# Fused attention, gated attention and mixer on one core: value products in fewer runs on parts of TensorE's array

## The chip, the cores and the metric

One NeuronCore of a Trainium2 chip runs the whole program. The metric is the device time of one execution in microseconds. A profiled execution also gives a trace, in which TensorE is called PE (its weight loads PEld), VectorE DVE, ScalarE ACT, GpSimd POOL and SyncE SP. All times of the trace count from the start of its span.

## The reference, cut to what matters

Three stages on 4 batches of 768 tokens, all in float32:

```python
# 1: attention in chunks of 32 queries, 8 heads of 64, context 16 left, 8 right, 8 memory tokens
scores = scale * np.matmul(q_c, k_full.transpose(0, 1, 3, 2))
a = softmax(scores);  out[:, :, c_start:c_end] = np.matmul(a, v_full)
# 2: 4 causal "expert" heads of 64 on x (768 x 512), each token keeps 2 of them by a gate
q = x @ wq[e];  k = x @ wk[e];  v = x @ wv[e]
a = softmax(where(causal, -1e9, scale * (q @ k.transpose(0, 2, 1))))
ye = a @ v @ wo[e];  out += mask * w * ye
# 3: mixer over tokens of rank 32, then a two-layer net 512 -> 2048 -> 512 with relu
u = x + (x.transpose @ U @ V).transpose;  return u + relu(u @ w_ch1) @ w_ch2
```

## The kernel before, in words

The program has an attention part (stages 1 and 2 and the mixer) and a dense part (the two-layer net). The change is in the attention part. The order of all instructions is made by a planner at build time: it takes the program's order as priorities and keeps a model of the engines' times. `tc.high_priority(AHEAD)` moves instructions up in that order.

**Local units.** Stage 1 is cut into 32 units (batch, pair of heads, half of the tokens). A unit is loaded by `local_load` (q_t, k_t, v_t on SP's queue), scored twice for three groups by `local_scores` (L533) and, one round later, turned by `local_turn` (L561, copied into `at` tiles at L563). `local_values` then makes its products with v_t, 12 calls that are 24 instructions of 64 columns each, and `local_split` copies the 128x384 result out of PSUM as xh (ACT) and xl (DVE), both at L580. These are the inputs of the projections of the next batch half.

**Rounds.** Stage 2 goes batch by batch through 12 rounds (list ROUNDS): a pair of expert heads pr and a block i of 128 queries, i = 0 to 2 for both pairs, then 3 to 5 for both. `rnd` writes one round: the load and the scores of a new unit, `scores` of the new block (L672, L674), `turn_scores` of the block before (transposes at L750, copied into `ath` tiles at L753), and one or two fillers. Fillers are `qk_proj` (L592), `v_proj` (L632), `mix_turn` (L778), `mix_up` (L808). Each round then ends in a "session": `local_values` of the unit turned in this round, `values` of the block turned in this round (products with v, 64 columns; in the first rounds of batch 0 and one of batch 3, by the table DELAY, of the block before it), and in some rounds `mix_down` (32 columns). All these matmuls are recorded by the helper `part` at L828, so that all have one line. The list `session` chains them in order and makes the first one wait for all copies that any of them reads. Behind it `keep` (L768) copies a block's 128x128 result into yT, and `mix_keep` the mixer's. `s_at` says in which round a unit is loaded, FILL and FILL0 how many fillers a round has.

**PSUM.** A tag is a set of PSUM tiles used in turn. Of the 8 banks of 2 KB, scores, transposes of scores and mix_turn use tag c (two tiles of two banks), local scores and turns tag lt (two banks), a session's results tag ts (one bank), and projections, mix_up and some spare tiles tag q (one bank). In a session's bank the unit's result stands in the first 384 columns and the block's in the last 128.

```python
TL, TE, TQ = dict(tag="lt", bufs=2), dict(tag="ts", bufs=1), dict(tag="q", bufs=1)
```

**The last batch** has no local units. Its rounds are filled by the first weights of the dense part and by `early`: two chunks of the dense net (`gemm1` L365, `gemm2` L382), whose results po stand in tags lt and q by turns.

Of the kernel before, what the change touches and what calls it, by code (L numbers as in the profile page):

```python
# [8 lines left out]
F32 = mybir.dt.float32  # L9
# [25 lines left out]
HALF = S // 2  # L35
# [4 lines left out]
WLOAD = {1: ((0,), ()), 2: ((1,), ()), 3: ((2, 3), ()), 5: ((), (0, 1))}  # L40
# [8 lines left out]
NKB = 2  # L49
NVB = 3  # L50
NLWK = 4
NLT = 3
NLA = 1
NAT = 6
DELAY = {0: (0, 1, 2, 3, 4, 5, 6, 7, 8), 3: (0,)}
NXP = 8
FS = 1
HG = 1
# [45 lines left out]
def tile_chunk_attention__moe_attention__mixer(  # L104
# [287 lines left out]
    def early(ps):  # L392

        for c in range(NEC):
            load_z(c)
            for f in range(FA):
                gemm1(ps, c, f, TL)
                yield
            for m in range(KT):
                po = ps.tile([128, 512], F32, name="po", **(TL if m % 2 else TQ))  # L400
                for f in range(FA):
                    gate = GATES.get(2 * m + f // 2) if c == NEC - 1 else None
                    with tc.issue_after(hold[gate]) if gate else ExitStack():
                        gemm2(po, c, f, m, f == FA - 1, f == 0)
                    if f % 2:
                        yield
                save_part(po, c, m)
            for f in range(FA):
                hs.pop((c, f))

    TC = dict(tag="c", bufs=2)
    TL, TE, TQ = dict(tag="lt", bufs=2), dict(tag="ts", bufs=1), dict(tag="q", bufs=1)
    ROUNDS = [(pr, i) for hf in range(2) for pr in range(2) for i in range(3 * hf, 3 * hf + 3)]
    with ExitStack() as p1:
        const = p1.enter_context(tc.tile_pool(name="const", bufs=1))
# [150 lines left out]
        def local_values(u, po):  # L566
            w = half[u]
            for qd in range(2):
                at = w["at"].pop(qd)
                for n in range(3):  # L570
                    g = qd * 3 + n
                    for j in range(2):
                        part(po[j * 64:(j + 1) * 64, g * GQ:(g + 1) * GQ], w["v"][:, g, j, :],
                                         at[:, n, j * 64:(j + 1) * 64], start=True, stop=True)
# [162 lines left out]
        turned_ins = {}  # L737
# [91 lines left out]

        def rnd(new=None, old=None, s_unit=None, o_unit=None, fill1=(), fill2=(), down=None, then=None, late=()):
            if s_unit:
                local_load(s_unit)
                if then:
                    load_weights(*then)
                local_scores(s_unit, 0)
            turned = []

            def between():  # L840
                if o_unit:
                    local_turn(o_unit, 0)
                turned.append(1)
            if new:
                scores(*new, between)
            if not turned:
                between()
            if s_unit:
                local_scores(s_unit, 1)
            if o_unit:  # L850
                local_turn(o_unit, 1)
            for f in fill1:
                f()
            if old:
                turn_scores(*old)
            for f in fill2:
                f()
            t = ps.tile([128, 512], F32, name="t", **TE) if o_unit or late else None
            places = [t[:, HALF:], t[:, :128]] if late else []
            with tc.high_priority(AHEAD):  # L860
                session.clear()
                behind = [x for v in late for x in turned_ins.pop(v)] + (half[o_unit]["ins"] if o_unit else [])
                if down:
                    pq = t if not o_unit else ps.tile([128, 512], F32, name="pq", **TQ)
                    behind += ys_ins.pop(down[:2])
                if o_unit:
                    local_values(o_unit, t[:, :HALF])
                for v, p in zip(late, places):
                    values(*v, p)
                if down:  # L870
                    mix_down(*down, pq)
                for x in behind:
                    tc.add_manual_dep(session[0], x.name, READY, reason="start of a run on parts of the array")
                for x, y in zip(session, session[1:]):
                    tc.add_manual_dep(y, x.name, QUEUE, reason="run on parts of the array")
            for v, p in zip(late, places):
                keep(*v, p)
            if o_unit:
                local_split(o_unit, t[:, :HALF])
            if down:  # L880
                mix_keep(*down, pq)

# [51 lines left out]
        for r in range(PRO):  # L934
            more = [lambda: qk_begin(0, 0, r - 2, pp)] if 2 <= r < KT + 2 else []
            if r == PRO - 1:
                more += [lambda t=t: v_proj(0, t) for t in range(3)]
            split = [lambda: split_weights(*WSPLIT[r])] if r in WSPLIT else []
            rnd(s_unit=units[r], o_unit=units[r - 1] if r else None, fill1=split, fill2=more, then=WLOAD.get(r))
            if r == 3:  # L940
                fetch_mixer()
            if r == 4:
                nc.vector.memset(rank_s, 0.0)
                nc.sync.dma_start(identb_s, identb)
                nc.sync.dma_start(tri_s, tri)
                nc.vector.memset(row_s[:, :S - 128], 0.0)
                nc.vector.tensor_copy(row_s[:, S - 128:], tri_s)
        load_mixer()
        old, mixed, turned = None, {}, []
        for b in range(B):  # L950
            last = b == B - 1
            s_at = {} if last else dict(zip(S_AT0 if b == 0 else S_AT, batch_half(b + 1, 0) + batch_half(b + 1, 1)))
            before = None
            if b == 0:
                s_at.update(zip(range(8), units[PRO:]))
                before = units[PRO - 1]
            work = pieces(b, 1) + ([] if last else pieces(b + 1, 0))
            for r, (pr, i) in enumerate(ROUNDS):
                n = (FILL0 if b == 0 else FILL)[r] if work else 0
                ending[0] = last and r >= 10  # L960
                now, work = work[:n], work[n:]
                f1, f2 = now[:1], now[1:]
                if b and r == (2 if last else 1):
                    f2 = f2 + [lambda: mix_turn(b - 1, 1)]
                if b and r == (4 if last else 7):
                    f1 = [lambda: mix_up(b - 1, 1)] + f1
                if r == 10:
                    f2 = f2 + [lambda: mix_turn(b, 0)]
                if b and r == 0 and not mixed.get(b - 1):
                    f1 = [lambda: mix_up(b - 1, 0)] + f1  # L970
                down = (b, 0) if r == 11 else (b - 1, 1) if b and r == 3 else None
                wait = r in DELAY.get(b, ())
                late = turned if wait or not old else turned + [old]
                turned = [old] if wait and old else []
                rnd((b, pr, i), old, s_at.get(r), s_at.get(r - 1) if r else before, f1, f2, down, late=late)
                old = (b, pr, i)
                if last:
                    if r == 0:
                        close_local()
                        behind_x.append(17)  # L980
                        with tc.issue_after(hold['q', 16]):
                            load_wt()
                        fuse = fuse_w1(ps, 0, TL)
                        fetch_w1()
                    if r < 6:
                        with tc.issue_after(hold['q', 16]) if r < 2 else ExitStack():
                            take(fuse, 2)
                    if r == 1:
                        fetch_w2()
                    if r == 3:  # L990
                        take(fuse, 99)
                        fuse_g = fill()
                    if 3 <= r < 6:
                        take(fuse_g, 1)
                    if r == 5:
                        close_proj()
            if last:
                rnd(None, old, late=[old])
                mix_turn(b, 1)
                mix_up(b, 0)  # L1000
                session.clear()
                pq = ps.tile([128, 512], F32, name="pq", **TE)
                mix_down(b, 1, pq)
                mix_keep(b, 1, pq)
                mix_up(b, 1)
                take(fuse_g, 999)
# [256 lines left out]
```

## Time and profile before

| | us |
|---|---|
| median of 3 runs | 819.76 (819.11 to 821.08) |
| profiled execution, whole | 821.44 |
| its span, first to last instruction | 819.0 |
| mean granted clock of TensorE | 0.994 |
| TensorE busy in the span | 794.0 |
| VectorE, ScalarE, GpSimd busy | 620.1, 499.4, 160.8 |

In a timeline a row is a group of like instructions: start, length from its first start to its last end, engine, line, tiles written and read, the weights' rows*columns, the shape, the count. A bracket gives the idle time ahead of it and what ended it. Matmuls overlap in the array: the start of each is recorded, its end is modelled, so one that follows closely starts before the end of the one before.

### The profile page before, as it was taken

Reading aid. Unit: us, or ns where it says so; the run is one execution under the profiler, and the core shown is the slowest. Engines: PE = TensorE matmul, PEld = TensorE weight load, DVE = VectorE, ACT = ScalarE, POOL = GpSimd, SP = SyncE. Lnnn points to the kernel's source line nnn. Section 1 sums busy time; section 2 is a strip of 40 time slices with the busy share of each in tenths; the row PEclk is TensorE's granted clock in tenths of the full one; section 3 lists DMA queues with packets and bytes.
Section 4 is the critical chain, followed back from the end, with each engine's and each line's share of the span. In section 5 each row is a group of like instructions: output and inputs, shape, how many; then the busy total and the mean of one; then the engine's idle time right before and its main releaser. Section 6 shows DMA issues by size and latency. Waiting matters only on the chain.

```text
span 819.0 us, 17878 instructions
## 1 busy us (share of the span) xinstructions
PE 794.0 (97%) x6382; PEld 713.1 (87%) x6382; DVE 620.1 (76%) x2029; ACT 499.4 (61%) x1448; POOL 160.8 (20%) x244
## 2 busy tenths in 40 slices
PE   8989999999999998999999999999999999999997
PEld 5779999798989897888788888999999999999996
DVE  6687767977767759959758799989587595885956
ACT  6787667776667646656445667665455564654652
POOL 4554443634233333422000000000000000000000
PEclk9999999999999999999999999999999999999999
DMA  9443343333223004123427635103003021030211
GB/s 290 128 139 110 101 128 95 122 106 95 67 89 106 27 9 185 62 94 112 142 77 242 196 129 180 53 1 111 19 2 129 1 93 37 1 130 1 78 52 52
DMA packets 36792, 77.67 MB, mean 95 GB/s; under 512 B 4192, under 2 KB 12896, under 8 KB 35936
## 3 DMA queue, kind: packets, MB, share of 16 engines
q1 hardware_dynamic: 36416, 76.21, 28.6%
q8 instruction: 50, 0.82, 0.4%
q14 instruction: 38, 0.31, 0.1%
q10 hardware_dynamic: 288, 0.32, 0.1%
HBM read 60.79 MB, written 15.73 MB: 93 GB/s over the span
## 4 chain that ended last, share of the span: by engine, by line
PE 75%; DVE 13%; ACT 5%; DMA 4%; issue 3%; POOL 0%; DVEq 0%; ACTq 0%; SPq 0%
PE acc L1136 24%; PE ph L365 15%; PE t L828 7%; PE pqk L592 6%; PE po L382 4%; PE tpc L750 4%; PE pv L632 4%; PE s L533 3%; DMA raw<-in_w 2%; PE sc L672 2%; PE sc L674 2%; PE tp L561 2%; DVE d_t L143 1%; ACT a L540 1%; DVE d_t L144 1%
## 5 line engine op out<-in xcount | busy, mean ns | idle before, releaser
L1136 PE MATMUL acc<-xhi,sw 128*128 128x256 f32 x1008 | 187.9, 282 | 0.1
L1136 PEld LDWEIGHTS acc<-xhi,sw 128*128 128x128 f32 x1008 | 159.3, 189 | 4.8 <-ACT xhi L1054 0.3
L1136 PE MATMUL acc<-xlo,sw 128*128 128x256 f32 x504 | 139.1, 282 | 0.2 <-DVE xlo L1055 0.2
L1051 DVE TENSOR_TENSOR sx<-t 128x256 f32<-128x256 f32 x180 | 67.7, 421 | 67.0 <-ACT t L1044 66.9
L1044 ACT ACTIVATE t<-ph 128x512 f32<-128x512 f32 x72 | 43.1, 598 | 100.5 <-PE ph L365 100.5
L1136 PEld LDWEIGHTS acc<-xlo,sw 128*128 128x128 f32 x504 | 95.5, 190 | 2.4 <-DVE xlo L1055 0.4
L730 POOL TENSOR_SCALAR ac<-ac,su,g 128x128 f32<-128x128 f32 (+5 forms) x92 | 70.4, 774 | 129.8 <-DVE su L728 73.9
L1054 ACT CAST xhi<-sx 128x256 fp32r<-128x256 f32 x205 | 74.8, 406 | 21.7 <-DVE sx L1051 19.0
L540 ACT ACTIVATE a<-a,nm 128x96 f32<-128x96 f32 x192 | 69.9, 366 | 15.7 <-DVE nm L537 15.2
L1055 DVE TENSOR_TENSOR xlo<-sx,xhi 128x256 fp32r<-128x256 f32 x205 | 76.7, 420 | 3.0 <-ACT xhi L1054 2.2
L695 ACT ACTIVATE ac<-ac,nmc 128x128 f32<-128x128 f32 (+5 forms) x72 | 47.8, 665 | 24.1 <-DVE nmc L693 23.7
L365 PE MATMUL ph<-zh,wp_l 128*128 128x512 f32 x192 | 61.4, 398 | 0.0
L365 PE MATMUL ph<-zh,wp_h 128*128 128x512 f32 x192 | 60.8, 394 | 0.0
L545 POOL TENSOR_TENSOR a<-a,rs 128x288 f32<-128x288 f32 x64 | 43.3, 679 | 76.3 <-DVE rs L544 12.7
L750 PE MATMUL tpc<-ident_s,ac 128*128 128x128 f32 x336 | 54.2, 286 | 3.5 <-DVE nmc L693 1.4
L533 PE MATMUL s<-k_t,q_t 128*128 128x96 f32 (+1 forms) x480 | 52.7, 272 | 3.9 <-DMA k_t<-in_kw 1.1
L365 PE MATMUL ph<-zl,wp_h 128*128 128x512 f32 x176 | 55.5, 394 | 0.0
L533 PEld LDWEIGHTS s<-k_t,q_t 128*128 128x128 f32 (+1 forms) x480 | 46.5, 174 | 9.1 <-issue 4.0
L750 PEld LDWEIGHTS tpc<-ident_s,ac 128*128 128x128 f32 x336 | 40.1, 146 | 11.4 <-issue 3.5
L693 DVE CUSTOM_DVE_ANT_0 ac<-sc,row_s 128x128 f32<-128x128 f32 (+5 forms) x72 | 42.8, 620 | 9.4 <-PE sc L674 8.5
L672 PE MATMUL sc<-kl,qs 128*128 128x384 f32 (+2 forms) x144 | 47.3, 334 | 2.1 <-DVE zf L354 1.0
L537 DVE CUSTOM_DVE_ANT_0 a<-s,band_s 128x96 f32<-128x96 f32 x192 | 39.4, 250 | 10.8 <-PE s L533 10.2
(209 smaller groups left out, 1950.2 us busy)
## 6 DMA issues: line engine op xcount, KB each, us to landing
raw<-in_w SPq DMA_DIRECT2D x42, 256.0 KB, 3.7
v_t<-in_vw SPq DMA_DIRECT2D x32, 288.0 KB, 3.3
q_t<-in_qT SPq DMA_DIRECT2D x24, 384.0 KB, 3.2
k_t<-in_kw SPq DMA_DIRECT2D x31, 220.0 KB, 3.5
part<-o SPq DMA_DIRECT2D x24, 256.0 KB, 3.1
pt<-part SPq DMA_DIRECT2D x6, 1024.0 KB, 4.8
out<-pt SPq DMA_DIRECT2D x24, 256.0 KB, 2.3
raw<-in_w SPq DMA_DIRECT2D x11, 512.0 KB, 4.0
```

Of the source, the lines that this page charges most:

```text
L365: nc.tensor.matmul(p, w[f // 4][:, pr, fs], z[:, pr], start=(n == 0), stop=(n == 5))
L533: last = nc.tensor.matmul(s[own, j, :], w["q"][own, qd * 3 + j], k_g[own], start=True, stop=True).ins
L540: nc.scalar.activation(a[:, j, :], a[:, j, :], AF.Exp, bias=nm[:, j:j + 1], scale=-1.0, accum_out=ss[:, j:j + 1])
L592: nc.tensor.matmul(p, w[:, kt, m * 128:(m + 1) * 128], x[b, kt, hf], start=(n == 0), stop=(n == 11))
L672: nc.tensor.matmul(s[:, o:o + w], q, kl[b, e, hf][:, :w], start=True, stop=False)
L730: (nc.vector if ending[0] else nc.gpsimd).tensor_scalar(aa[h][:, :n], aa[h][:, :n], su[:, h:h + 1], gates[b, i // 3][:, i % 3, 2 * pr + h: ...
L750: hold['t', 6 * (i // 3) + 3 * pr + i % 3] = nc.tensor.transpose(tp[h][:, j * 128:(j + 1) * 128], aa[h][:, j * 128:(j + 1) * 128], ident_s ...
L828: session.append(nc.tensor.matmul(*a, **kw).ins)
L1051: nc.vector.tensor_tensor(x, t[:, p[0], p[1]], t[:, q[0], q[1]], op=op)
L1054: nc.scalar.copy(hi, x)
L1055: nc.vector.tensor_sub(lo, x, f32(hi))
L1136: ended[0] = nc.tensor.matmul(acc[n][:, m], w[:, ms], x, start=(f == FA and u == 0 and m == 0), stop=(f == NF - 2 and u == 2 and m == 1)).ins
```

## The change

Sessions no longer stand in every round. A table SESSIONS says which rounds of a batch have one. Units that were turned since the last session are gathered in `locs`, blocks in `turned`; a session takes them together, up to two units and three blocks, and a block that was turned in the session's own round is left for the next one, except in the rounds of the table FRESH. A session with two units, or with a unit and more than one further product, takes two banks. Tags ts and q become one tag of two banks, which sessions, projections, mix_up and spare tiles use in turn. po of `early` now uses tag lt alone. There are 8 ath tiles in place of 6 and 5 at tiles in place of 3. The mix_turn of the batch before moves from round 1 to round 2.

```diff
-NLT = 3
+NLT = 5
-NAT = 6
-DELAY = {0: (0, 1, 2, 3, 4, 5, 6, 7, 8), 3: (0,)}
+NAT = 8
+SESSIONS = {0: (0, 2, 4, 6, 8, 9, 11), 1: (1, 3, 5, 7, 9, 11), 2: (1, 3, 5, 7, 9, 11), 3: (1, 3, 5, 7, 9, 11)}
+FRESH = ((0, 9), (1, 9), (2, 9), (3, 9), (3, 11))
...
-                po = ps.tile([128, 512], F32, name="po", **(TL if m % 2 else TQ))
+                po = ps.tile([128, 512], F32, name="po", **TL)
...
-    TL, TE, TQ = dict(tag="lt", bufs=2), dict(tag="ts", bufs=1), dict(tag="q", bufs=1)
+    TL, TE, TQ = dict(tag="lt", bufs=2), dict(tag="ts", bufs=2), dict(tag="ts", bufs=2)
...
-            t = ps.tile([128, 512], F32, name="t", **TE) if o_unit or late else None
-            places = [t[:, HALF:], t[:, :128]] if late else []
+            if not (locs or late or down):
+                return
+            free = [ps.tile([128, 512], F32, name="t", **TE)]
+            if len(locs) == 2 or locs and len(late) + bool(down) > 1:
+                free.append(ps.tile([128, 512], F32, name="t2", **TQ))
+            pos = [x[:, :HALF] for x in free[:len(locs)]]
+            places = [x[:, o:o + 128] for n, x in enumerate(free) for o in ((HALF,) if n < len(locs) else (HALF, 256, 128, 0))]
             with tc.high_priority(AHEAD):
                 session.clear()
-                behind = [x for v in late for x in turned_ins.pop(v)] + (half[o_unit]["ins"] if o_unit else [])
+                behind = [x for v in late for x in turned_ins.pop(v)] + [x for u in locs for x in half[u]["ins"]]
                 if down:
-                    pq = t if not o_unit else ps.tile([128, 512], F32, name="pq", **TQ)
                     behind += ys_ins.pop(down[:2])
-                if o_unit:
-                    local_values(o_unit, t[:, :HALF])
-                for v, p in zip(late, places):
-                    values(*v, p)
+                kept = [(v, places.pop(0)) for v in late]
+                for n in range(max(len(locs), 1)):
+                    if locs:
+                        local_values(locs[n], pos[n])
+                    for v, p in kept[n:n + 1] if n + 1 < len(locs) else kept[n:]:
+                        values(*v, p)
                 if down:
+                    pq = places.pop(0)
                     mix_down(*down, pq)
...
-            for v, p in zip(late, places):
+            for v, p in kept:
                 keep(*v, p)
-            if o_unit:
-                local_split(o_unit, t[:, :HALF])
+            for u, p in zip(locs, pos, strict=True):
+                local_split(u, p)
...
-                if b and r == (2 if last else 1):
+                if b and r == 2:
                     f2 = f2 + [lambda: mix_turn(b - 1, 1)]
...
-                wait = r in DELAY.get(b, ())
-                late = turned if wait or not old else turned + [old]
-                turned = [old] if wait and old else []
-                rnd((b, pr, i), old, s_at.get(r), s_at.get(r - 1) if r else before, f1, f2, down, late=late)
+                o_unit = s_at.get(r - 1) if r else before
+                locs += [o_unit] if o_unit else []
+                now, wait = turned, [old] if old else []
+                if (b, r) in FRESH:
+                    now, wait = now + wait, []
+                if r in SESSIONS[b]:
+                    rnd((b, pr, i), old, s_at.get(r), o_unit, f1, f2, down, late=now, locs=locs)
+                    turned, locs = wait, []
+                else:
+                    rnd((b, pr, i), old, s_at.get(r), o_unit, f1, f2)
+                    turned = turned + [old] if old else turned
```

## Rows read from the trace of the kernel before

**Rows 1.** The page: TensorE's busy time, and the chain that ended last, by engine.
```profile
PE 794.0 (97%) x6382; PEld 713.1 (87%) x6382; DVE 620.1 (76%) x2029; ACT 499.4 (61%) x1448; POOL 160.8 (20%) x244
...
PE 75%; DVE 13%; ACT 5%; DMA 4%; issue 3%; POOL 0%; DVEq 0%; ACTq 0%; SPq 0%
```

**Rows 2.** Stretches: bounds, length, busy time of each engine, clock, DMA share, GB/s.
```profile
125.00:215.00 90.00, 86.98 (x860) 79.98 (x859) 68.97 (x316) 63.35 (x231) 39.89 (x60) 0.98 0.34 104
215.00:312.00 97.00, 93.71 (x926) 85.99 (x925) 68.37 (x287) 63.15 (x202) 34.54 (x55) 0.98 0.20 65
```

**Rows 3.** PE's timeline: the first and the last of the runs of L828.
```profile
13.94 0.92 PE L828 MATMUL t<-at,v_t 96*64 96x64 f32 x24
...
418.92 0.85 PE L828 MATMUL pq<-y,u_s 128*32 128x128 f32 x12
```

**Rows 4.** PE's timeline: into a run and out of it into a projection.
```profile
267.21 0.28 PE L672 MATMUL sc<-kl,qs 128*128 128x256 f32 x1
267.33 0.28 PE L674 MATMUL sc<-kd,qs 128*128 128x256 f32 x1
267.54 0.92 PE L828 MATMUL t<-at,v_t 96*64 96x64 f32 x24
...
269.04 0.97 PE L592 MATMUL pqk<-xl,wqk_h 128*128 128x384 f32 x4
269.85 0.87 PE L592 MATMUL pqk<-xh,wqk_h 128*128 128x384 f32 x4
```

**Rows 5.** PE's timeline: a run of value products alone, and mix_down by itself.
```profile
136.42 1.53 PE L828 MATMUL t<-ath,vt 128*64 128x128 f32 x24
137.88 0.33 PE L750 MATMUL tpc<-ident_s,ac 128*128 128x128 f32 x1
138.05 0.49 PE L561 MATMUL tp<-ident_s,a 128*96 128x128 f32 x3
...
139.11 0.85 PE L828 MATMUL pq<-y,u_s 128*32 128x128 f32 x12
```

**Rows 6.** Timeline of all engines: the end of a run and the emptying of its bank.
```profile
207.39 1.48 PE L828 MATMUL t<-ath,vt 128*64 128x128 f32 x24
...
208.80 0.39 PE L632 MATMUL pv<-wvg_h,xl 128*128 128x260 f32 x1
...
208.92 0.27 ACT L768 COPY yT<-t 128x128 f32<-128x128 f32 x1
...
209.08 0.48 ACT L580 CAST xh<-t 128x384 fp32r<-128x384 f32 x1
...
209.60 0.56 DVE L580 TENSOR_TENSOR xl<-t,xh 128x384 fp32r<-128x384 f32 x1 [1.55 <-ACT xh L580]
```

**Rows 7.** PE's waits, 40 to 420 us: who, for what, total us, times, longest.
```profile
PE pz L808 <- DVE qs L612: 1.0, 2, 0.5
...
PE pz L808 <- DVE z L809: 0.8, 2, 0.7
PE t L828 <- DVE ath L753: 0.8, 3, 0.3
PE t L828 <- ACT ath L753: 0.6, 1, 0.6
...
PE pqk L592 <- DVE qs L612: 0.2, 1, 0.2
```

**Rows 8.** Stretches where the granted clock falls; the columns of rows 2.
```profile
194.00:196.00 2.00, 1.76 (x10) 1.51 (x10) 2.00 (x10) 1.49 (x5) 0.00 (x0) 0.71 0.50 72
196.00:198.00 2.00, 2.00 (x12) 2.00 (x11) 1.88 (x8) 1.98 (x7) 1.10 (x2) 0.50 0.78 298
...
284.00:286.00 2.00, 2.00 (x11) 2.00 (x11) 1.19 (x3) 1.64 (x4) 0.00 (x0) 0.50 0.00 0
```

**Rows 9.** PE's timeline: mix_up's two products, with the idle time ahead of each.
```profile
281.96 0.41 PE L808 MATMUL pz<-v_st,qm 96*128 96x384 f32 x1 [0.55 <-DVE qs L612]
283.02 0.45 PE L808 MATMUL pz<-v_st,qm 96*128 96x384 f32 x1 [0.65 <-DVE z L809]
```

More of the change, by code (lines that the diff above doesn't have):

```diff
@@ L828, in part, with rnd @@
             session.append(nc.tensor.matmul(*a, **kw).ins)
-        def rnd(new=None, old=None, s_unit=None, o_unit=None, fill1=(), fill2=(), down=None, then=None, late=()):
+        def rnd(new=None, old=None, s_unit=None, o_unit=None, fill1=(), fill2=(), down=None, then=None, late=(), locs=()):
             if s_unit:
@@ L938, in tile_chunk_attention__moe_attention__mixer @@
             split = [lambda: split_weights(*WSPLIT[r])] if r in WSPLIT else []
-            rnd(s_unit=units[r], o_unit=units[r - 1] if r else None, fill1=split, fill2=more, then=WLOAD.get(r))
+            rnd(s_unit=units[r], o_unit=units[r - 1] if r else None, fill1=split, fill2=more, then=WLOAD.get(r), locs=units[r - 1:r] if r else ())
             if r == 3:
@@ L948, in tile_chunk_attention__moe_attention__mixer @@
         load_mixer()
-        old, mixed, turned = None, {}, []
+        old, mixed, turned, locs = None, {}, [], []
         for b in range(B):
@@ L960, in tile_chunk_attention__moe_attention__mixer @@
                 ending[0] = last and r >= 10
-                now, work = work[:n], work[n:]
-                f1, f2 = now[:1], now[1:]
-                if b and r == (2 if last else 1):
+                f1, f2, work = work[:n][:1], work[:n][1:], work[n:]
+                if b and r == 2:
                     f2 = f2 + [lambda: mix_turn(b - 1, 1)]
@@ L997, in tile_chunk_attention__moe_attention__mixer @@
             if last:
-                rnd(None, old, late=[old])
+                rnd(None, old, late=turned + [old])
                 mix_turn(b, 1)
```

## The prediction

> **What bounds the kernel now.** The page comes first. TensorE (PE) is busy 97% of the span and the chain that ended last is 75% PE, 13% VectorE (DVE), 5% ScalarE (ACT) [rows 1]: time goes only if PE has less to do or waits less. Next comes the table of stretches: in the two middle batches DVE works 68.97 of 90 us and 68.37 of 97 us [rows 2], so it can't hide everything that is moved onto it. PE itself is idle there for 3.0 and 3.3 us only, so there is little waiting to win; the list of PE's waits between 40 and 420 us, the attention part, which is all that the change touches, names it [rows 7]. What can be won must lie inside PE's "busy" time; for that, third, I read PE's timeline instruction by instruction, by starts, since ends are modelled. The value products (L828) use 64 or 32 columns of the array; what stands around them in the rounds uses 128. In the timeline they stand in 55 unbroken runs, of which the first and the last are shown [rows 3].
>
> **What a run costs at its two ends.** Going in: between two 128-column score products of 256 columns the distance is 0.12 us (267.21 to 267.33), from the last of them to the run 0.21 (267.33 to 267.54) [rows 4]: +0.09. First pair: 24 value products at the head of a run take 1.53 us [rows 5], 24 that follow local products inside a run 1.48 [rows 6]: +0.05. Going out: in the latter run the last product started 0.27 us (its own length) before the end of the row, at 208.60, and the next full product at 208.80, 0.20 later [rows 6]; inside the run the distance from pair to pair is (1.48 - 0.28) / 11 = 0.109, all but 0.01 of it behind the second of a pair: +0.10. First product after it: four pqk products take 0.97 us just after a run and 0.87 otherwise [rows 4], +0.10; where transposes follow, the first takes 0.17 (137.88 to 138.05) against (0.49 - 0.27) / 2 = 0.11 [rows 5], +0.06. So one run costs 0.30 to 0.34 us beyond its products, on the engine that sets the end.
>
> **The change part by part.** *Fewer runs.* Before, there are 5 runs in the prologue, 47 in the rounds (round 0 of the last batch has none), 2 at the end; the trace has one more because batch 0's mix_down stands alone at 139.11 [rows 5]. After: 5, then 7 + 6 + 6 + 6 = 25, then 2, that is 32. The products are the same ones. 23 runs fewer x 0.325 = -7.5 us (bounds: 23 x 0.30 = 6.9 and 23 x 0.34 = 7.8, if all of it reaches the end). A second local unit behind value products in one run has no switch: both use 64 columns, and the join local-to-value is already inside today's runs.
>
> *One tag of two banks in place of two tags of one.* Today projections, mix_up and spare tiles share one bank. PE's waits for that bank to be emptied are pz on DVE qs 1.0 us, pz on DVE z 0.8, pqk on DVE qs 0.2 [rows 7]: 2.0 in all. With two banks the next tile takes the other one: -1.6, a fifth left for the times when a run has the other one (bounds -2.0 and 0).
>
> *New waits for banks.* By the lists SESSIONS and FRESH, 17 of the 25 runs take both banks (those with two local units, or one and two or more other products). A projection that comes right behind such a run must now wait until a bank is empty; today it has its own. The run whose value products start at 207.39 shows the size: its matmuls end at 208.87, pv starts at once in its own bank, and the run's bank is empty at 209.60 + 0.56 = 210.16 [rows 6], 1.29 us later. Worst case 17 x 1.29 = 21.9 us. Against it: the first of two banks is read while the second is filled, so at the end of the run it is nearly empty; and PE has transposes, scores and local scores of the next round in other banks. The nearest rows are those of the single bank today: by the code 64 tiles go through it in the rounds (28 pqk, 24 pv, 12 pz) and cost 2.0 us of waiting, 0.03 each [rows 7]. I take 0.12 per two-bank run, four times that because two banks go at once: +2.0 (bounds 0 and 21.9).
>
> *Waits at the head of a run.* Products of a round are now mostly taken one or two rounds late, so their copies are long done. Today PE waits for them 0.8 + 0.6 us [rows 7]; round 9 and the last one keep the old order: -0.5 (bounds -1.4 and 0).
>
> *More bunched emptying.* A two-bank run leaves two xh and two xl and up to three yT copies at a time on ACT and DVE (0.48, 0.56 and 0.27 us [rows 6]) where two rounds shared them. The sum of work is the same. Where DVE is already full, 2.00 of 2.00 us at 194 to 196 [rows 8], PE's gain turns into waiting; of the 7.5 us I let a tenth go: +0.7 (bounds 0 and 3.0, if in the two middle batches with 12 of the 23 runs three quarters of a run's price were lost).
>
> *po takes both banks of the tag lt.* It had a bank of the projections' tag for every other tile. One po is 12 products of about 0.23 us, 2.7 us, and its emptying lies beside the next one's filling: at 512 columns about 0.48 x 512 / 384 = 0.64 us, an estimate from the 384-column copy [rows 6]. 8 tiles, +0.3 (bounds 0 and 8 x 0.64 = 5.1). *mix_turn a round later, eight ath and five at tiles:* all copies stay, the consumer mix_down is still in round 3, and the loads of v_t, now held up to two rounds, have three tiles in rounds of some 7.5 us (12 rounds in about 90 [rows 2]): 0. If a tile of v_t came free late, its load would hold the next q_t and k_t behind it on SP's queue, and PE would wait at local scores; [rows 7] has no such wait today.
>
> Sum: -7.5 - 1.6 + 2.0 - 0.5 + 0.7 + 0.3 = -6.6 us. The profiled execution took 821.44 us (819.0 span, 2.4 around it) and would take 814.8. It lies 1.7 above the median of the runs, 819.76, which gives 819.8 - 6.6 = 813.2.
>
> **The Trainium skill against the change.** The rows say that a run's bank is empty 1.29 us after its end and that PE goes on meanwhile [rows 6]. The Trainium skill, page "TensorEngine Tiling (Array Packing)", section "PSUM Bottleneck", says that parts of the array speed up the matmuls but not the emptying of PSUM, so that the copies can become the bound. By that rule longer runs with two banks would stand behind their copies. Today's trace does not show it: the view of [rows 7] has no wait of PE for yT, xh or xl. It is the rule behind the next two rivals.
>
> **Rivals.** *Eaten.* Each two-bank run costs PE 0.45 us of waiting for a bank: 17 x 0.45 = 7.7 in place of 2.0, total -0.9, 818.9. For it: projections do stand right behind runs now [rows 4, 6]. Against: the other banks' work. Chance 0.14.
>
> *Slower.* The same place, with the price that a busy bank had at its worst: pz waited 0.65 us for it at 283.02 [rows 9]. 17 x 0.65 = 11.1, less the other terms' -8.6: +2.5, 822.3. It decides from 8.6 / 17 = 0.51 us per run. For it: this wait was with one bank taken, here it is both. Against: it stood where DVE was overloaded, and occurred twice in 12 pz. Chance 0.14.
>
> *The clock too.* The granted clock is 0.50 at 196 to 198 and at 284 to 286 us [rows 8], 1.2 in place of 2.4 GHz, the second time just after PE had been idle for the pz waits (0.55 and 0.65 us, at 281.96 and 283.02 [rows 9]). At half clock 2.0 us and, at a mean of 0.71, another 2.0 x 0.29 / 0.5 = 1.2 us: 3.2, half of it lost, 1.6 each. If the second bank takes these waits away and the clock stays up, -3.2 more: 810.0. Against: DVE is full there anyway, and a new wait can lower the clock elsewhere. Chance 0.12.
>
> *It doesn't do what it says.* The chain that orders a run forbids nothing in between: batch 0's mix_down was torn off its run [rows 5]. If ten of the 25 runs break in two because their second bank comes late, 13 switches go in place of 23: 3.3 less gain, 816.5. Chance 0.10.
>
> **How the numbers follow.** Forecast 0.50, own range 811 to 815.8. About 0.2% (1.6 us) is what a measurement can tell from none, so faster means under 818.1, slower over 821.4. Faster: 0.50 + 0.12 + 0.10 and a little of "eaten", 0.73; same 0.13; slower 0.14. The range for 8 in 10 takes in the clock's case below and "eaten" above: 809.0 to 820.5; "slower" is left out, with the far end of the clock's case.
>
> **What would show it.** Right: 32 or 33 runs of L828, each with the same prices at its ends; the last run, at 418.92 now [rows 3], earlier by 5 to 8 us, the part behind it as long as before; pz waits gone. Wrong: PE waiting on xl, xh or yT at pqk or pv; runs cut in two; new stretches of 0.50 in the clock. If the runs are 32 and the time has not moved, the price of a run's ends was covered by waits on DVE, and my reading by starts was wrong.

## The result, and the profile after

The changed kernel takes 813.89 us (median of 5 runs, 811.13 to 814.40) against 819.76 before (5 runs): 5.9 us less by the medians, ratio 0.9912 with a 95% interval of 0.9886 to 0.9938. The forecast was 813.2. The profiled execution took 814.0, its span 811.9 against 819.0.

The page of the changed kernel, the lines of [rows 1]:

```profile
PE 784.9 (97%) x6382; PEld 710.2 (87%) x6382; DVE 620.5 (76%) x2029; ACT 497.2 (61%) x1448; POOL 159.4 (20%) x244
...
PE 70%; DVE 16%; ACT 6%; DMA 5%; issue 3%; POOL 0%; DVEq 0%; ACTq 0%; POOLq 0%; SPq 0%
```

The count of PE's instructions is the same, 6382, and PE's busy time is 9.1 us shorter. Where it went shows best when the span is cut at three events: the first score product of batch 0, the first mask product of the last batch (L680, in the kernel before L679), and the last product on parts of the array. Stretches of the kernel before, with the columns of [rows 2]:

```profile
46.41:313.38 266.97, 257.68 (x2582) 237.46 (x2579) 197.47 (x894) 186.27 (x650) 110.60 (x171) 0.99 0.31 96
313.38:419.50 106.12, 102.23 (x738) 84.01 (x737) 82.15 (x171) 61.08 (x145) 26.14 (x33) 1.00 0.31 106
419.50:818.97 399.47, 393.10 (x2600) 359.53 (x2595) 309.10 (x808) 220.47 (x531) 0.00 (x0) 1.00 0.23 80
```

The same stretches of the changed kernel:

```profile
46.49:305.32 258.83, 251.16 (x2590) 234.78 (x2587) 196.91 (x885) 183.98 (x648) 110.46 (x174) 0.99 0.32 95
305.32:412.68 107.36, 100.41 (x730) 84.35 (x729) 83.23 (x173) 61.40 (x145) 25.16 (x30) 1.00 0.33 115
412.68:811.88 399.20, 392.97 (x2600) 359.35 (x2594) 308.86 (x808) 220.30 (x531) 0.00 (x0) 1.00 0.23 80
```

Batches 0 to 2 became 8.1 us shorter, the last batch 1.2 us longer, and the part behind it kept its length. The last run ends 6.8 us earlier (419.50 to 412.68), as forecast. The number of runs is not as forecast: PE's timeline has 44 runs of L829 (L828 before), not 32. Twelve of the 17 two-bank runs stand in two pieces. One of them, in the timeline of the changed kernel (PE's rows, and the last read of the projection pv that stood in the tag before this run):

```profile
74.01 0.92 PE L829 MATMUL t<-at,v_t 96*64 96x64 f32 x24
74.75 0.61 PE L829 MATMUL t<-ath,vt 128*64 128x128 f32 x8
...
74.90 0.16 DVE L636 COPY lg<-pv 128x4 f32<-128x4 f32 x1
...
75.29 0.54 PE L562 MATMUL tp<-ident_s,a 128*96 128x128 f32 x3
75.58 0.42 PE L673 MATMUL sc<-kl,qs 128*128 128x384 f32 x1
...
76.19 0.51 PE L751 MATMUL tpc<-ident_s,ac 128*128 128x128 f32 x3
76.54 0.36 PE L534 MATMUL s<-k_t,q_t 128*128 128x96 f32 x2
76.83 0.92 PE L829 MATMUL t<-at,v_t 96*64 96x64 f32 x24
77.58 0.83 PE L829 MATMUL t<-ath,vt 128*64 128x128 f32 x12
```

The session of round 4 of batch 0 starts with its first unit and block, then transposes and scores come in for 1.5 us, then the second unit and block follow: two entries and two exits, as two separate sessions would have. Yet in this execution the second bank was not late: pv had been read out at 75.06, before the row of the first half ended (75.36). It is the same in seven of the twelve: every earlier tile of the tag had been emptied before the first half ended; in two more it took up to 0.3 us longer, in three 1.2 to 3.5 us. The order was fixed at build time by the planner, on its own model of the times. Why that model put other work between the halves of those seven is not shown.

PE's waits of the changed kernel, 40 to 420 us, with the columns of [rows 7]:

```profile
PE tpc L751 <- POOL ac L731: 2.6, 4, 1.2
PE tpc L751 <- DVE nmc L694: 1.2, 2, 1.1
PE t L829 <- DVE y L782: 1.2, 2, 0.9
...
PE pz L809 <- DVE qm L799: 1.1, 2, 0.6
...
PE t L829 <- DVE ath L754: 0.4, 2, 0.3
...
PE t L829 <- DVE qs L613: 0.3, 1, 0.3
```

The waits of pz for the bank of another tile (DVE qs and DVE z in [rows 7]) are gone, as forecast; pz now waits for its own input qm. No wait for xl, xh or yT, which the prediction had named as a sign of being wrong, is in the list. In the attention part the granted clock fell to half once (170.3 to 173.7 us) in place of twice.

### The profile page after: what moved, and what is told of

Read it like the earlier page. It is cut to its first block, busy times and chain, and to the rows that moved or that the text cites. A ratio compares the mean times of both kernels' runs of the same rounds, so it can differ in the third digit from the quotient of the medians.

```text
span 811.9 us, 17863 instructions
## 1 busy us (share of the span) xinstructions
PE 784.9 (97%) x6382; PEld 710.2 (87%) x6382; DVE 620.5 (76%) x2029; ACT 497.2 (61%) x1448; POOL 159.4 (20%) x244
## 4 chain that ended last, share of the span: by engine, by line
PE 70%; DVE 16%; ACT 6%; DMA 5%; issue 3%; POOL 0%; DVEq 0%; ACTq 0%; POOLq 0%; SPq 0%
PE acc L1150 25%; PE ph L366 14%; PE t L829 6%; PE pqk L593 5%; PE pv L633 3%; PE s L534 3%; PE po L383 3%; PE tpc L751 3%; DMA raw<-in_w 2%; PE sc L673 2%; PE sc L675 2%; PE tp L562 2%; ACT a L541 2%; DVE d_t L144 1%; DMA part<-o 1%
```

## The experiments

All are timed against the kernel before on the same chip; kernels of one block shared a chip. The number of runs is that of the order of PE's instructions.

| kernel | runs | median us | ratio to before, 95% |
|---|---|---|---|
| changed | 44 | 813.89 | 0.9912 (0.9886 to 0.9938) |
| e1_tags | 55 | 838.46 | 1.0225 (1.0205 to 1.0245) |
| e2_group | 44 | 848.45 | 1.0346 (1.0325 to 1.0367) |
| e3_every | 56 | 815.62 | 0.9950 (0.9934 to 0.9967) |
| e4_price | 55, 25 of them interrupted | 830.83 | 1.0127 (1.0109 to 1.0145) |
| e5_whole | 32 | 816.69 | 0.9972 (0.9958 to 0.9985) |
| e6_po | 45 | 828.78 | 1.0111 (1.0088 to 1.0135) |
| e7_tags_po | 54 | 819.32 | 0.9995 (0.9981 to 1.0010) |
| e8_late | 53 | 825.59 | 1.0080 (1.0059 to 1.0101) |
| e9_last | 51 | 811.14 | 0.9892 (0.9869 to 0.9915) |
| e10_first | 49 | 816.49 | 0.9960 (0.9944 to 0.9976) |
| e11_sizes | 55 | 815.56 | 0.9948 (0.9929 to 0.9967) |
| changed_again | 44 | 813.18 | 0.9919 (0.9897 to 0.9941) |

Already the first two columns say that the count of runs alone doesn't order the times: 32 runs are slower than 51.

**First block: what is a run's end worth, and which part of the change holds the gain?**

e1_tags is the kernel before with

```diff
-    TL, TE, TQ = dict(tag="lt", bufs=2), dict(tag="ts", bufs=1), dict(tag="q", bufs=1)
+    TL, TE, TQ = dict(tag="lt", bufs=2), dict(tag="ts", bufs=2), dict(tag="ts", bufs=2)
```

> The kernel before with one edit: tags ts and q become one tag of two banks. Sessions stay as they were, 55 runs of L828. Theory A (the gain is the ends of the runs that went, 0.30 to 0.34 us each): no run goes, so only the waits for the projections' bank can go, at most 2.0 us: 817.8 to 819.8. Theory B (the gain is the second bank for projections and mix_up, and the half-clock stretches that follow their waits): most of the gain is here, 814 to 816.

Both theories missed: 838.46. Its stretches from the last batch on:

```profile
308.81:413.02 104.21, 85.31 (x636) 70.17 (x635) 76.61 (x163) 54.61 (x135) 24.35 (x31) 0.93 0.24 82
413.02:837.77 424.75, 417.53 (x2700) 379.66 (x2696) 317.36 (x819) 227.21 (x541) 0.00 (x0) 1.00 0.24 80
```

The last batch ends early, but it holds 636 matmuls in place of 738, and PE is idle 18.9 us of it (104.21 - 85.31); the part behind has 100 matmuls more and is 25 us longer. Dense work that filled the gaps of the last batch was pushed behind it.

e2_group is the changed kernel with the two old tags (the edit above undone).

> The changed kernel with its tags as before: ts and q are two tags of one bank each, a session's second bank comes from q. The order of its instructions has 44 runs, as the changed kernel's. Theory A: 11 runs fewer than before x 0.325 = 3.6 us and the rest of what the changed kernel won by fewer waits at heads of runs: 814 to 816.5. Theory B: without the common tag the gain is gone, 818.5 to 820.5.

848.45, far worse than either. PE's waits of this kernel, 40 to 420 us:

```profile
PE pqk L593 <- DVE z L810: 4.8, 3, 2.1
PE t L829 <- DVE kl L619: 4.7, 2, 2.3
```

Projections wait for a bank that mix_up holds, and sessions for one that a projection holds. In batches 0 to 2 PE is idle for 28.9 us, in the changed kernel for 7.7. So these two-bank sessions need the common tag; one-bank groups with the old tags were not run.

e3_every is the changed kernel with

```diff
-SESSIONS = {0: (0, 2, 4, 6, 8, 9, 11), 1: (1, 3, 5, 7, 9, 11), ...
+SESSIONS = {b: tuple(range(12)) for b in range(4)}
```

> The changed kernel with a session in every round (SESSIONS holds all 12 rounds): one unit and the block of the round before, no grouping; common tag, eight ath and five at tiles, po on lt stay. 56 runs in its order. Theory A: no run goes, 818.5 to 820.5. Theory C (the gain is that value products come a round late and find their copies done, and that the tags are common): 813.5 to 816.

815.62: with 56 runs, one more than before, the kernel keeps more than half of the gain (0.50 of 0.88%). The time is the one that theory C gave, and it speaks against theory A as the main cause. The mechanism that theory C names for the late products, copies that are done, is not seen in the trace: at the heads of its runs PE waits for ath at least as long as before (0.8 and 0.6 us in [rows 7]):

```profile
PE t L829 <- DVE ath L754: 1.4, 4, 0.6
PE t L829 <- ACT ath L754: 0.6, 1, 0.6
```

e4_price is the kernel before with, ahead of `values` where a unit's products stand in front,

```diff
+                    if o_unit:
+                        part(p[:, :32], identb_s, tri_s[:, :32], start=True, stop=True)
                     values(*v, p)
```

> The kernel before with one 128-column bf16 matmul of 32 columns (result overwritten) put between the local products and the value products of the 25 runs that hold both: 25 changes out of and into parts of the array more. Theory A: each costs 0.30 to 0.34 us and 0.03 for the matmul: 25 x 0.36 = +9.0, 827.5 to 830. Rival D (the ends of a run are covered by waits of DVE and ACT, so the trace's distances don't reach the end): under +4, 820 to 823.5.

830.83. PE's timeline of it:

```profile
223.83 0.92 PE L828 MATMUL t<-at,v_t 96*64 96x64 f32 x24
224.69 0.19 PE L828 MATMUL t<-tri_s,identb_s 128*128 128x32 bf16 x1
224.80 1.09 PE L828 MATMUL t<-ath,vt 128*64 128x128 f32 x16
```

From the first local product to the first value product it is 0.97 us. In the kernel before, the step is 0.75 (267.54 to 268.29):

```profile
267.54 0.92 PE L828 MATMUL t<-at,v_t 96*64 96x64 f32 x24
268.29 0.83 PE L828 MATMUL t<-ath,vt 128*64 128x128 f32 x12
```

With the first pair's +0.05 of the prediction that is 0.27 us by starts. At the end 25 interruptions cost 0.0127 x 820 = 10.4 us (8.9 to 11.9), 0.42 each (0.36 to 0.48), the inserted matmul included: a little above theory A's figure, and more than the starts show. Rival D falls: what the distances show reaches the end. The rest is not the switch alone: in its trace batches 0 to 2 are 10.7 us longer (277.65 against 266.97), of which PE is busy for 7.7 and idle for 3.0, and the clock fell to half there three times in place of twice. The inserted matmul also has another type (bf16 among fp32); what a change of type costs by itself was not tested.

**Second block: why do 56 runs win nearly as much as 44, and what do whole runs bring?**

e5_whole is the changed kernel with a list `evac` of the readers of the common tag's tiles, and

```diff
+                if len(free) > 1:
+                    behind += evac[-8:]
                 for x in behind:
                     tc.add_manual_dep(session[0], x.name, READY, reason="start of a run on parts of the array")
```

> The changed kernel with one edit: a session of two banks starts only when the readers of the last tiles of the common tag are done, so that nothing gets between its two halves. The order of its instructions has 32 runs in place of the changed kernel's 44. Theory A (run ends are the price): 12 x 0.33 to 0.43 us less, 809 to 810.5 by the changed kernel's 813.9. Rival G (runs were broken because the second bank was not free, and PE now pays that as a wait): 813 to 817.

816.69, slower than the changed kernel (the intervals of the ratios don't meet) and in rival G's range. Its stretches, and two of its waits:

```profile
46.37:307.09 260.72, 248.09 (x2535) 234.25 (x2533) 194.94 (x882) 183.32 (x643) 110.58 (x174) 0.99 0.31 94
307.09:416.90 109.81, 104.24 (x783) 88.49 (x783) 83.81 (x176) 62.94 (x151) 26.55 (x30) 0.98 0.34 114
```

```profile
PE t L830 <- DVE kl L620: 3.3, 2, 2.5
PE sc L674 <- ACT ac L700: 2.0, 1, 2.0
```

In batches 0 to 2 PE is idle for 12.6 us (260.72 - 248.09) in place of the changed kernel's 7.7. It is also busy 3.1 us less (248.09 against 251.16), but with 55 matmuls fewer, which moved to the last batch, so this is not a measure of the run ends. The clock falls to half three times for 3.4 us, once of these in the last batch, instead of once, and part of the loss goes with it: at a granted clock of 0.994 and 0.995 five executions have spans of 813.1 to 816.4 us, two of the changed kernel at 0.994 have 812.4 and 812.6. The edit also makes a run wait at its start for both banks. A run that starts as soon as its first bank is free, with its second half right behind, was not tried.

e6_po is the changed kernel with

```diff
-                po = ps.tile([128, 512], F32, name="po", **TL)
+                po = ps.tile([128, 512], F32, name="po", **(TL if m % 2 else TQ))
```

> The changed kernel with po taking tags lt and the common tag by turns, as before lt and q. The trace of the run with common tags alone had its last run of L828 at 413.0 us, earlier than before, but the part behind it 25 us longer. Theory H (po holds a bank of the common tag for long in the last batch, so that dense work is pushed behind the attention part): 825 to 840. Theory A alone says nothing happens: 813 to 815.

828.78, as theory H has it. Its stretches from the last batch on show the picture of e1_tags:

```profile
307.26:404.28 97.02, 80.76 (x628) 67.24 (x627) 75.71 (x163) 54.52 (x134) 23.66 (x30) 0.98 0.29 103
404.28:828.71 424.43, 416.52 (x2700) 378.63 (x2696) 317.60 (x819) 227.07 (x541) 0.00 (x0) 1.00 0.23 80
```

e7_tags_po is the kernel before with the edit of e1_tags and the po line of the change.

> The kernel before with two edits: one common tag of two banks, and po on lt alone. Sessions as before, in every round and at once; 54 runs in its order. Theory F (what the kernel with a session in every round won, 4.4 us, comes from the second bank): 814.5 to 817. Theory E (it comes from taking value products a round late): 818 to 820.5.

819.32, no change. But its stretches move against each other:

```profile
46.29:307.63 261.34, 253.50 (x2582) 235.33 (x2579) 195.95 (x887) 185.46 (x648) 111.19 (x173) 0.99 0.33 100
307.63:418.77 111.14, 103.67 (x737) 85.12 (x737) 82.73 (x172) 60.89 (x146) 26.02 (x32) 0.98 0.29 96
```

Batches 0 to 2 win 5.6 us by the second bank, the only edit that acts there; the last batch loses 5.0. Most likely that is the price of po on one tag, but the common tag acts in the last batch too, and no run separates the two there.

e8_late is the kernel before with

```diff
-DELAY = {0: (0, 1, 2, 3, 4, 5, 6, 7, 8), 3: (0,)}
+DELAY = {0: tuple(range(9)), 1: tuple(range(8)), 2: tuple(range(8)), 3: tuple(range(8))}
```

and the change's NLT, NAT and mix_turn in round 2.

> The kernel before with value products taken a round late in rounds 0 to 7 of all batches (DELAY), eight ath and five at tiles, mix_turn in round 2; two tags of one bank, po by turns, as before; 53 runs in its order. Theory E: 814.5 to 817. Theory F: 818.5 to 820.5.

825.59, slower by 0.8%: theory E alone falls too. Batches 0 to 2 take 270.64 us, and PE's longest waits of it are

```profile
PE pz L808 <- DVE qs L612: 2.4, 1, 2.4
...
PE pz L808 <- DVE z L809: 1.6, 2, 0.8
```

for the single bank again, 4.0 us where [rows 7] have 1.8. Late products win only together with the common tag (e3_every), and lose without it. That the bank's waits are the whole of the loss isn't shown. Nor are the two kernels late in the same rounds: e3_every takes products late in rounds 8, 10 and 11 too.

**Third block: where does grouping win?**

e9_last and e10_first are the changed kernel with

```diff
+SESSIONS = {0: EVERY, 1: EVERY, 2: EVERY, 3: (1, 3, 5, 7, 9, 11)}      # e9_last
+SESSIONS = {0: (0, 2, 4, 6, 8, 9, 11), 1: ODD, 2: ODD, 3: EVERY}       # e10_first
```

where EVERY stands for all 12 rounds and ODD for (1, 3, 5, 7, 9, 11).

> The changed kernel with sessions grouped in the last batch alone (its 6 sessions have no units and need one bank); in batches 0 to 2 one session in every round. 51 runs in its order, 5 fewer than with a session in every round everywhere (815.6). Theory J (grouping wins where it needs one bank, and the two-bank groups win nothing because their halves stand apart): 813 to 814.5, as good as the changed kernel or better. Theory A (only the count of runs matters, 0.33 us each): between, 815.6 - 5 x 0.33 = 814.0; J and A part on the next kernel.

> The counterpart: sessions grouped in batches 0 to 2, one in every round in the last batch. 49 runs in its order, 7 fewer than with a session in every round. Theory A: 815.6 - 7 x 0.33 = 813.3. Theory J: 815 to 816.5, no gain from two-bank groups.

e9_last 811.14, under both theories' figures; e10_first 816.49, at the upper end of theory J and far from theory A's 813.3. The kernel with a session in every round that ran beside them (e11_sizes, below) takes 815.56. So two-bank groups win nothing, and theory J holds. Stretches of e9_last, then of e10_first:

```profile
46.01:302.99 256.98, 251.20 (x2590) 233.44 (x2588) 196.18 (x885) 185.24 (x647) 110.94 (x174) 1.00 0.33 98
302.99:410.09 107.10, 100.00 (x729) 84.05 (x728) 82.50 (x172) 61.48 (x147) 26.21 (x31) 1.00 0.31 110
```

```profile
48.26:307.17 258.91, 251.21 (x2589) 234.78 (x2587) 196.20 (x885) 184.11 (x648) 110.92 (x174) 0.99 0.32 95
307.17:417.30 110.13, 102.32 (x729) 84.35 (x729) 81.99 (x173) 60.72 (x145) 24.96 (x30) 1.00 0.32 113
```

In the last batch, grouped sessions need one bank and stay whole: 107.10 against 110.13 us, with PE busy 2.3 us less (100.00 and 102.32) by 5 fewer runs, 0.46 each. In e3_every the last batch takes 109.46 us and PE is busy for 101.45; against that it is 0.29 each. In batches 0 to 2 a session in every round gives 256.98 us, grouping 258.91; one half-clock stretch lies in the latter. At full clock in this part the changed kernel's second measurement, changed_again, gives

```profile
46.36:304.34 257.98, 249.78 (x2590) 233.50 (x2587) 196.46 (x885) 183.92 (x648) 110.91 (x174) 1.00 0.31 95
```

Against e9_last PE is busy 1.4 us less (249.78 and 251.20), by 7 fewer runs, and idle 2.4 us more (257.98 - 249.78 = 8.2, and 5.8). In this pair of executions two-bank groups give back what they save.

e11_sizes is e3_every with the old sizes:

```diff
-NLT = 5
+NLT = 3
...
-NAT = 8
+NAT = 6
```

> The kernel with a session in every round and value products a round late, with six ath and three at tiles as before the change. 55 runs in its order. Theory E (value products a round late win because their copies are done, and that needs the tiles): the four to six ath tiles that wait leave too few for the next transposes, 817 to 820. Rival K (the tiles don't matter, the order does): 815 to 816.5.

815.56, rival K: without grouping the additional tiles do nothing, and the part of theory E that needs them falls.

> The changed kernel once more, beside these three on one chip: 813 to 814.5 if nothing but noise lies between the jobs.

813.18, so the jobs agree. e9_last lies 2.0 us below it on the same chip; four of its five runs are in 810.94 to 811.27 and one is 809.51, the changed kernel's six go from 810.78 to 814.65. The intervals of the two ratios overlap: e9_last beats the kernel before by 1.1% (0.85 to 1.3) and has the lowest median of the kernels run, but much of its lead over the changed kernel goes with the clock: at a granted clock of 1.000 its spans are 807.7 and 809.3 us, those of changed_again 808.9 and 809.9.

## Why the prediction was right in time and where its steps failed

The time (813.2 forecast, 813.89 measured) and the side are right; the sum -6.6 met -5.9. That the sum fits is luck: the largest term, the fewer runs, was put far too high, the common tag too low, and the two errors cancelled.

**Fewer runs, -7.5.** The price per run held roughly: forecast 0.30 to 0.34 us, measured 0.42 at the end (0.36 to 0.48, e4_price, with idle time and clock in it) and 0.29 to 0.46 in PE's busy time of the last batch. The count didn't. The step "After: 5, then 7 + 6 + 6 + 6 = 25, then 2, that is 32" is true of the sessions and false of the runs, of which there are 44: the rival "It doesn't do what it says" came true in its count (11 runs went, it had 13), though not in its time (816.5). The cause that it named, a second bank that comes late, is shown by the trace for five of the twelve cuts at most; at the other seven the bank was empty in time, and the order came from the planner's model. Made whole by waiting at their start, the runs are slower (e5_whole); no kernel that was run has them whole without that wait. As planned, two-bank groups win nothing (e10_first 816.49, e11_sizes beside it 815.56), where the prediction expected most of its gain from them. One-bank groups in the last batch do win: 110.13 to 107.10 us for 5 fewer runs.

**One tag of two banks, -1.6.** Mis-sized. In batches 0 to 2 the second bank takes 266.97 to 261.34 us (e7_tags_po), 5.6. Part of it is the clock of these two executions: two half-clock stretches of 3.4 us became one, some 1.7 us as an estimate from their length. PE's idle time fell by 1.5 us only (9.3 to 7.8), about what the term had counted from [rows 7]; the rest lies in PE's busy time (257.68 to 253.50), and what made that shorter is not shown.

**Waits at the head of a run, -0.5.** PE's waits for ath there fell from 1.4 to 0.4 us, but 1.2 for y, the input of mix_down, and 0.3 for qs are new: 1.9 in all, so the term came out with the other sign. And the order of the products is worth more than these waits, and not additive: products a round late cost 6.6 us with the old tags (e8_late 825.59, the kernel before beside it 819.02), while e3_every is 3.7 faster than e7_tags_po (815.62 and 819.32, by medians of two blocks). Between these two also lies mix_turn in round 2; which of the two wins, and by which wait, is open. I had costed the edits singly.

**po on lt, +0.3.** Most likely mis-sized: the last batch of e7_tags_po is 5.0 us longer, near the upper bound of 5.1, though the common tag acts there too; part of that is one half-clock stretch (317.5 us), again some 1.7. What I missed wholly is that this edit can't be left out: with po on the common tag, dense work is pushed behind the attention part and 15 us are lost (e6_po).

**New waits, +2.0, and bunched emptying, +0.7.** In batches 0 to 2 grouping raises PE's idle time from 5.8 to 8.2 us (e9_last, changed_again), 2.4 for both terms together, near the forecast 2.7. But PE's waits there have none for xl, xh or yT, so the size came out and the mechanism isn't shown. The rival "Eaten" did not come: it had 0.45 us for each two-bank run, and 2.4 / 17 is 0.14. The Trainium skill (page "TensorEngine Tiling (Array Packing)", section "PSUM Bottleneck") has the emptying of PSUM as what can become the bound. No run here shows it: the 3.3 us that the whole runs of e5_whole wait for kl are the emptying of a projection's tile, not of the run's own.

**The clock too.** One of the two half-clock stretches went in the profiled execution. But executions at equal clock show that the gain does not come from there: at a granted clock of 1.000 four executions of the kernel before, in the three blocks, have spans of 816.1 to 816.9 us, four of the changed kernel 808.9 to 810.7. That is some 6.7 us, no less than between the medians. The -3.2 that this rival had on top did not come.

## What to carry to other kernels

A switch of the array's tiling has a price that can be read from starts in the timeline, here as a lower bound: 0.27 us by starts, 0.42 at the end (e4_price). But count the runs in the order that the planner makes, not in the source: a session that needs a second PSUM bank was cut in two in 12 of 17 cases, one that needs a single bank stayed whole. Group first where one bank will do. Edits that share a PSUM tag are to be costed together: here the common tag (with po moved) won nothing, late products alone lost, and together they won more than half of the gain (e7_tags_po, e8_late, e3_every). A tile that stays open for long (po) doesn't belong in a tag that short tiles rotate through.

## What the runs showed that I had not expected

One long-lived tile in a tag that short tiles rotate through moved 100 matmuls out of the last batch and made the part behind it 25 us longer (e1_tags, e6_po). And the granted clock varies between executions of one kernel: the changed kernel's five runs have spans of 809.1 and 810.7 us at a granted clock of 1.000 and 812.4 at 0.994, so 2 to 3 us of a difference between two single executions can go with the clock.
